# Two small pads that move the start addresses of an adaLN, convolution and bilinear-GLU kernel's tiles

## The chip, the cores and the metric

The kernel runs on one core of one Trainium2 chip. The metric is the device time of one execution in microseconds, the median of three runs. The core has five engines with queues of their own: TensorE (PE in the profile, and PEld for the loading of its stationary operand), VectorE (DVE), ScalarE (ACT), GpSimd (POOL) and SyncE (SP), which issues most of the transfers.

## The reference

The input `x` is `A_u`, 2048 tokens of 640 channels in float32. Six rows of 640 (`sa, ca, ga, sb, cb, gb`) come from a conditioning vector.

```python
mod = (_silu(c) @ w_mod).reshape(c.shape[0], 6, 1, -1)
h = _layernorm(x, axis=-1) * (1 + ca) + sa
x = x + ga * _A_ref(h, ...)      # a long convolution over the tokens, by FFT
h = _layernorm(x, axis=-1) * (1 + cb) + sb
x = x + gb * _B_ref(h, ...)      # ((h @ w_gate) * (h @ w_up)) @ w_down, 1536 wide
```

`_A_ref` builds, for each channel, a kernel of 2048 taps from 192 complex modes, and convolves the tokens with it (padded to 4096, by FFT), plus `u * Dskip`. `_B_ref` is the gated unit without a nonlinearity.

## The kernel before

The kernel has two stages on one program. The first, to about 433 us, builds the convolution's kernels (GpSimd, ScalarE and VectorE make sines, cosines and products, line 651 and line 733; TensorE sums over the modes, lines 747 and 762) and does the FFTs on TensorE (lines 784 to 939). The second, from about 507 us, is the gated unit. Between them lie the last channels and the first layer norms of the second stage.

The order of all instructions is written out by hand: `SCHED` holds the due time of each piece of the first stage, and the loops at the end of `tile_kernel` hold the order of the second. A tile of memory is taken from pools. Pools on the left side are stacked upwards, those opened with `side="right"` downwards from the top of the memory. `const` is the first pool on the left, so every later left tile begins above it: first `pk` and `pk1` (the kernel-generation tiles `EQ`, `LQ`, `RH`, `Pha`, `QtA` and others), and, when those are closed, `wp`, which `mk` takes from for the second stage (`xb`, `wga`, `wgb`, `wur`, `wsgh`, `wsgl`, `hh1`, `hl1`, `e` and some `a` tiles). On the right lie first the convolution's tiles (`t_tw`, `t_ti`, `shr`, `oneR`, `f16`, `gh`, `hf` and others), and, when these are closed, the pool `gp`, whose tiles are all taken at once in one loop (line 1336).

In the second stage the precision of float32 is made of pairs: `hilo` (line 994 and, on ScalarE, line 135) splits a value into a high part and a rest, each of type fp32r, whose names end in `h` and `l`. A product of two such pairs is three matmuls per block: high by high, rest by high, high by rest. There are two kinds of products, and each matmul loads its own 128 x 128 stationary operand (PEld) and then streams its moving operand:

- `prod` (line 1030): 512 tokens wide. Moving are the activations, stationary the weights. The gate and up projections share partial sums, so that each loop over one of 12 feature blocks has seven products: `y_1` (6 matmuls), `z_1` (9), `x_1` (6), `y_2` (6), `x_2` (9), `y_3` (9) and `z_2` (9), 54 in all, for 1024 tokens in two operands of 512. There are two halves with 12 such loops each. `x_1` and `x_2` read `hh1`, `hl1` (activations) and `wsgh`, `wsgl` (weights); the others read `sh`, `sl`, `hh2`, `hl2` and `wth`, `wtl`, `wsuh`, `wsul`. Two `x` products stand apart, in `u_gate` (line 1164), before the first loop. The trace leaves out buffer numbers, so `hh` in it is `hh1` or `hh2`.
- `down` (line 1457): the down projection, four blocks of 512 tokens with 12 steps each. A step has 24 matmuls, in turn 384 and 256 columns wide. Moving are the weights, in `wsgh` and `wsgl`; stationary are the activations, split into `e` for steps 0 and 1 of blocks 0 and 2, and else into parts of `sh`, `sl`, `hh2`, `hl2`, which are free again by then (`d_prep`, from line 1424 on).

```python
def prod(ps, ks):
    for n, (a, b) in enumerate(((0, 0), (1, 0), (0, 1))):
        for m, (w, k, x, l) in enumerate(ks):
            PE.matmul(ps, w[a][:, k], x[b][:, l], start=n == 0 and m == 0, stop=n == 2 and m == len(ks) - 1)
```

```python
if m < 2:
    AH[tb, f] = tuple(mk("e", [P, 512], F32, 4).bitcast(F32R) for _ in range(2))
```

While block 1 runs, transposes of the next tokens (line 1110) stand between its steps. Line 804 in the first stage is a matmul of fp32r tiles as well: `shr` and `oneR`.

Of the kernel before, what the change touches and what calls it, by code (L numbers as in the profile page):

```python
# [10 lines left out]
F32 = mybir.dt.float32  # L11
F32R = mybir.dt.float32r
# [7 lines left out]
P = 128  # L20
# [109 lines left out]
def tile_kernel(ctx: ExitStack, tc: tile.TileContext, I, out):  # L130
# [6 lines left out]
    const = ctx.enter_context(tc.tile_pool(name="const", bufs=1))  # L137
# [15 lines left out]
    for k in range(11):  # L153
        V.memset(shl[:, k : k + 1], k + 1)
    colT = const.tile([P, 10], F32, name="colT")
    ry = const.tile([P, 24], F32, name="ry")
    ry, rv = ry[:, 0:16], ry[:, 8:24]

    slot = {k: iter(v) for k, v in SLOT.items()}
# [1176 lines left out]
    for n, sh_, dt_, b_ in ([(f"a{j}", [P, 512], F32, 1) for j in range(10, 15)] + [(n, [P, 512], F32, 1) for n in TMP]  # L1336
                            + [(n, [P, 3, 512], F32R, 1) for n in H2] + [(n, [P, 9, 512], F32R, 1) for n in SX]
                            + [("tf", [P, 8, P], F32, 1), ("wth", [P, 8, P], F32R, 2), ("wtl", [P, 8, P], F32R, 2), ("wsuh", [P, 4, P], F32R, 2),
                               ("wsul", [P, 4, P], F32R, 2)] + [(f"a{j}", [P, 512], F32, 1) for j in (*range(5), *range(15, 24))]):
        FIRST[n] = gp.tile(sh_, dt_, name=n, bufs=b_)  # L1340
    ps_a = ctx.enter_context(tc.tile_pool(name="ps_a", bufs=1, space=PSUM))

# [284 lines left out]
```

## Time and profile before

| | us |
|---|---|
| median of three runs (lowest, highest) | 966.64 (965.85, 967.36) |
| the profiled execution | 967.17 |
| its span, first to last instruction | 965.3 |
| mean granted clock of TensorE | 0.976 |

Times in the views of the trace count from the span's start. In rows of the timeline, the first number is the start and the second the length of a run of like instructions; the lengths of matmuls overlap, since the next one starts while the last one drains, so that the pitch of matmuls is read from starts, not from lengths. In the chain in order of time the numbers are start and length of a piece of the chain that ended last.

### The profile page before, as it was taken

How to read it: one execution, taken by the hardware profiler on the slowest of the kernel's cores; microseconds unless marked ns; L12 is line 12 of the kernel's file. 1: busy time of each engine (PE TensorE's matmuls, PEld its weight loads, DVE VectorE, ACT ScalarE, POOL GpSimd, SP SyncE). 2: the span in 40 equal slices, each digit the busy share in tenths (PEclk: the TensorE clock that was granted, in tenths of full speed). 3: DMA queues.
4: the chain of work that ended last, by engine and by line, in shares of the span. 5: the costliest groups of instructions: out<-in, count | busy, mean ns of one | idle time of the engine just before them, and what ended most of it. 6: DMA issues, size and time to landing. Idle time of an engine off the chain costs nothing.

```text
span 965.3 us, 26463 instructions
## 1 busy us (share of the span) xinstructions
PE 867.6 (90%) x11070; PEld 719.7 (75%) x11070; DVE 746.2 (77%) x1301; ACT 575.9 (60%) x1088; POOL 568.1 (59%) x419
## 2 busy tenths in 40 slices
PE   3877887898798789889889999999999999999998
PEld 1665655676575467678567888899998888889998
DVE  7996687889789967887899777795677877677452
ACT  7899988887987979754773222235555222224330
POOL 5998999799799989940125766721021544451000
PEclk9978999999999889999999999999999999999999
DMA  8496575534465645468853355155536222213241
GB/s 302 153 305 220 163 235 187 135 122 126 122 189 166 178 118 156 137 206 265 226 162 110 108 191 171 48 197 158 192 137 218 83 82 82 82 55 90 74 165 55
DMA packets 141320, 148.94 MB, mean 154 GB/s; under 512 B 8208, under 2 KB 119568, under 8 KB 139792
## 3 DMA queue, kind: packets, MB, share of 16 engines
q1 hardware_dynamic: 139904, 145.80, 48.3%
q8 instruction: 87, 1.43, 0.6%
q10 hardware_dynamic: 1296, 1.44, 0.4%
q14 instruction: 33, 0.27, 0.1%
HBM read 108.36 MB, written 38.86 MB: 153 GB/s over the span
## 4 chain that ended last, share of the span: by engine, by line
PE 47%; DVE 5%; ACT 1%; issue 1%; DMA 1%; DVEq 0%; SPq 0%; ACTq 0%
PE pa L1030 28%; PE pa L1457 16%; PE psg L1030 1%; DMA wgb<-B_w_gate 1%; DVE st L1083 1%; DVE sl L994 1%; PE psg L1164 1%; PE psg L1110 0%; PE psg L1457 0%; DVE a L1149 0%; ACT wsgh L135 0%; ACT hh L135 0%; ACT xb L135 0%; DVE xb L1470 0%; DVE wsgl L994 0%
## 5 line engine op out<-in xcount | busy, mean ns | idle before, releaser
L651 POOL TENSOR_TENSOR EQ<-LQ,RH 128x1536 f32<-128x1536 f32 x40 | 124.3, 3108 | 0.2
L135 ACT ACTIVATE z<-pa 128x512 f32<-128x512 f32 x24 | 14.4, 599 | 169.2 <-PE pa L1030 121.9
L994 DVE TENSOR_TENSOR wsgl<-wga,wsgh 128x640 fp32r<-128x640 f32 x72 | 70.4, 981 | 47.9 <-ACT wsgh L135 47.9
L135 ACT ACTIVATE wsgh<-wga 128x640 fp32r<-128x640 f32 x72 | 52.3, 732 | 66.1 <-PE pa L1457 34.7
L1401 POOL TENSOR_TENSOR z<-z,s 128x512 f32<-128x512 f32 x24 | 34.2, 1426 | 89.7 <-DVE s L1400 89.7
L1006 POOL TENSOR_TENSOR tf<-wur,wgb 128x256 f32<-128x256 f32 x24 | 19.0, 790 | 97.7 <-DVE wtl L994 58.8
L651 POOL TENSOR_TENSOR EP<-LP,RH 128x768 f32<-128x768 f32 x40 | 65.8, 1655 | 10.2 <-DVE PtB L733 10.2
L1457 PE MATMUL pa<-wsgh,sh 128*128 128x384 f32 (+1 forms) x295 | 69.6, 314 | 0.0
L1457 PE MATMUL pa<-wsgl,sh 128*128 128x384 f32 (+1 forms) x295 | 69.2, 312 | 0.0
L1457 PE MATMUL pa<-wsgh,sl 128*128 128x384 f32 (+1 forms) x295 | 69.2, 312 | 0.0
L651 POOL TENSOR_TENSOR Pha<-LH,DH 128x1536 int32<-128x1536 int32 (+1 forms) x21 | 62.5, 2977 | 0.5 <-ACT tra L135 0.3
L651 POOL TENSOR_TENSOR Phb<-LH,DH 128x1536 int32<-128x1536 int32 x20 | 62.4, 3118 | 0.0
L733 DVE TENSOR_TENSOR QtA<-tra,EQ 128x1024 f32<-128x1024 f32 x44 | 51.9, 1215 | 9.8 <-ACT tra L135 6.8
L994 DVE TENSOR_TENSOR wtl<-tf,wth 128x256 fp32r<-128x256 f32 (+1 forms) x72 | 59.0, 845 | 0.0
L733 DVE TENSOR_TENSOR QtA<-trb,EQ 128x1024 f32<-128x1024 f32 x36 | 42.7, 1217 | 10.3 <-ACT trb L135 8.0
L1399 DVE TENSOR_TENSOR s<-pa,s 128x512 f32<-128x512 f32 x24 | 16.6, 690 | 43.9 <-PE pa L1030 38.9
L762 PE MATMUL kg<-QtB,PtB 64*32 64x64 f32 x2560 | 46.3, 222 | 4.5 <-issue 2.0
L762 PEld LDWEIGHTS kg<-QtB,PtB 64*32 64x32 f32 x2560 | 39.2, 110 | 12.4 <-issue 5.3
L1457 PEld LDWEIGHTS pa<-wsgh,sl 128*128 128x128 f32 x295 | 45.7, 188 | 0.0
L1457 PEld LDWEIGHTS pa<-wsgl,sh 128*128 128x128 f32 x295 | 45.7, 188 | 0.0
L1457 PEld LDWEIGHTS pa<-wsgh,sh 128*128 128x128 f32 x295 | 45.7, 188 | 0.0
L1030 PE MATMUL pa<-sh,wtl 128*128 128x512 f32 x144 | 44.9, 393 | 0.8 <-DVE wtl L994 0.8
(650 smaller groups left out, 2853.5 us busy)
## 6 DMA issues: line engine op xcount, KB each, us to landing
wga<-wdg SPq DMA_DIRECT2D x24, 640.0 KB, 4.3
wga<-B_w_gate SPq DMA_DIRECT2D x12, 640.0 KB, 5.9
wgb<-B_w_gate SPq DMA_DIRECT2D x24, 320.0 KB, 3.4
wur<-B_w_up SPq DMA_DIRECT2D x24, 320.0 KB, 4.0
xb<-x2d SPq DMA_DIRECT2D x6, 1280.0 KB, 8.5
t_ti<-w_mod SPq DMA_DIRECT2D x3, 1600.0 KB, 8.8
t_tw<-w_mod SPq DMA_DIRECT2D x3, 1600.0 KB, 10.4
WD<-Wa SPq DMA_DIRECT2D x8, 512.0 KB, 3.1
```

The costliest lines, as they stand in the source:

```text
L135: return S.activation(o, i, f, **kw)
L651: G.tensor_tensor(o.rearrange("p x (h l) -> p x h l", l=8), lo.unsqueeze(2).to_broadcast([P, rows, nh, 8]), hi.rearrange("p h x -> p x h") ...
L733: V.tensor_tensor(t, tr, e.unsqueeze(1).to_broadcast([P, 2, R, 32]), op=OP.mult)
L762: PE.matmul(kg[j * 32 : j * 32 + 32, dd, :], PtB[lo : lo + 64, c, r, :], QtB[lo : lo + 64, c, r, :], start=False, stop=dd == 7 and c == 1, ...
L994: V.tensor_tensor(lo, v, hi, op=OP.subtract)
L1006: G.tensor_tensor(t[:, 0:2], u[:, 0:2], g[:, 0:2], op=OP.subtract)
L1030: PE.matmul(ps, w[a][:, k], x[b][:, l], start=n == 0 and m == 0, stop=n == 2 and m == len(ks) - 1)
L1083: V.bn_stats(st[:, i, k, :], XB[tb][:, i, k * P : k * P + P])
L1164: PE.matmul(UX[i], WS[i][a][:, k], HX[0][b][:, k], start=k in (0, 2) and n == 0, stop=k in (1, 4) and n == 2)
L1399: V.tensor_tensor(S67[i], ps, S6[i], op=OP.add)
L1401: G.tensor_tensor(ZT[i], ZT[i], S67[i], op=OP.add)
L1457: PE.matmul(ACC[tb][t][c], x[:, ts], w[:, cs], start=st, stop=f == NF - 1 and n == 2 and (one or t % 2 == 1))
```

## The change

The tile `ry` in `const` grows from 24 to 48 float32 values per partition, 96 bytes more; its users read the same columns. A tile `gap` of 96 bytes is added at the end of the list of tiles of `gp`. Nothing reads or writes it.

```diff
@@ -153,7 +153,7 @@
     colT = const.tile([P, 10], F32, name="colT")
-    ry = const.tile([P, 24], F32, name="ry")
+    ry = const.tile([P, 48], F32, name="ry")
     ry, rv = ry[:, 0:16], ry[:, 8:24]
@@ -1336,7 +1336,7 @@
-                               ("wsul", [P, 4, P], F32R, 2)] + [(f"a{j}", [P, 512], F32, 1) for j in (*range(5), *range(15, 24))]):
+                               ("wsul", [P, 4, P], F32R, 2)] + [(f"a{j}", [P, 512], F32, 1) for j in (*range(5), *range(15, 24))] + [("gap", [P, 24], F32, 1)]):
         FIRST[n] = gp.tile(sh_, dt_, name=n, bufs=b_)
```

In the built programs the tiles begin, within a partition, at these bytes. The large tiles of a group agree modulo 128, those of the second stage modulo 256 too.

| tiles | before | after | modulo 128 (modulo 256) |
|---|---|---|---|
| left, first stage: `EQ`, first buffer | 38816 | 38912 | 32 (160) to 0 (0) |
| left, second stage: `wsgh`, first buffer | 45472 | 45568 | 32 (160) to 0 (0) |
| left, second stage: `hh1`; `e`, first buffer | 67232; 93856 | 67328; 93952 | 32 (160) to 0 (0) |
| `gp`: `sh` | 135136 | 135040 | 96 (224) to 0 (128) |
| `gp`: `wth`, first buffer | 176096 | 176000 | 96 (224) to 0 (128) |
| right, first stage: `shr` | 192576 | 192576 | 64 (64), unchanged |

## Prediction

> **What bounds the kernel now.** I read the page first, for its span and for the lines of the chain that ended last.
>
> ```profile
> span 965.3 us, 26463 instructions
> PE pa L1030 28%; PE pa L1457 16%; PE psg L1030 1%; DMA wgb<-B_w_gate 1%; DVE st L1083 1%; DVE sl L994 1%; PE psg L1164 1%; PE psg L1110 0%; PE psg L1457 0%; DVE a L1149 0%; ACT wsgh L135 0%; ACT hh L135 0%; ACT xb L135 0%; DVE xb L1470 0%; DVE wsgl L994 0%
> ```
>
> The chain lies on TensorE, in the products of the gate and up projections (line 1030, `prod`) and in the down projection (line 1457, `down`). Next I read the busy times by stage, cut where the chain changes line. The columns are PE, PEld, DVE, ACT, POOL, the granted clock, the DMA share and GB/s.
>
> ```profile
> 0.00:433.00 433.00, 348.11 (x7820) 265.78 (x7821) 360.16 (x625) 367.75 (x695) 387.09 (x247) 0.95 0.58 178
> 507.00:637.00 130.00, 129.51 (x567) 106.37 (x568) 103.49 (x148) 37.61 (x85) 85.25 (x76) 1.00 0.41 134
> 637.00:730.00 93.00, 92.71 (x631) 91.89 (x630) 67.70 (x143) 49.48 (x81) 18.16 (x15) 1.00 0.46 153
> 730.00:875.00 145.00, 145.00 (x636) 119.02 (x635) 111.20 (x164) 45.76 (x101) 64.74 (x63) 1.00 0.31 100
> 875.00:962.00 87.00, 86.33 (x577) 86.09 (x576) 40.69 (x64) 27.05 (x44) 1.31 (x2) 1.00 0.31 99
> ```
>
> The convolution stage (0 to 433 us) is shared: GpSimd is busiest (387 of 433 us), ScalarE and VectorE close behind. From 507 us to the end TensorE is busy without a pause, at the full granted clock, and DVE and GpSimd have room. TensorE's own waits from 507 to 960 us are these two in total:
>
> ```profile
> PE pa L1030 <- DVE s L1387: 0.8, 1, 0.8
> PE psg L1110 <- ACT xb L135: 0.3, 1, 0.3
> ```
>
> So in that half no transfer and no other engine decides the time, only how fast one matmul follows another. A faster VectorE, ScalarE or DMA there is worth nothing.
>
> **What the change moves.** No instruction, no wait and no shape changes; the order on each engine is the same, and only buffer numbers in names shift by one. What changes are start addresses, and the built program has them as the change says. Taken modulo 128, the tiles of the left stack (from the kernel-generation tiles to `xb`, `wga`, `wsgh`, `wsgl`, `hh1`, `hl1`, `e`) go from 32 to 0, and the tiles of the pool `gp` (`sh`, `sl`, `hh2`, `hl2`, `wth`, `wtl`, `wsuh`, `wsul`) from 96 to 0. The convolution's right-hand tiles stay at 64. Two things change for TensorE: the absolute start, and the offset between left and right tiles, which was 64 bytes and is now none (128 modulo 256).
>
> *Absolute start.* A start of 64 modulo 128 already occurs: `shr` and `oneR` in line 804 are fp32r tiles with 512 columns, as in line 1030. The first pair of matmuls after a pause shows the pitch of the first: here line 804 (start 64), then line 1164 (both operands at 32).
>
> ```profile
> 106.87 0.50 PE L804 MATMUL psfc<-shr,oneR 128*128 128x512 f32 x1 [1.08 <-ACT f16b L135]
> 107.20 0.40 PE L804 MATMUL psfb<-shr,oneR 128*128 128x512 f32 x1
> ```
> ```profile
> 488.49 0.50 PE L1164 MATMUL psg<-hl,wsgh 128*128 128x512 f32 x1 [1.33 <-DVE hl L1151]
> 488.82 0.39 PE L1164 MATMUL psg<-hh,wsgh 128*128 128x512 f32 x1
> ```
>
> Both are 0.33 us. A start at 64 instead of 32 buys a matmul nothing; I price the absolute start at 0. A start at 0 with such an operand is in no row, so this can fail (third rival).
>
> *Offset of the two tiles, in the down projection.* Each of its 48 steps (24 matmuls) reads the weights `wsgh`, `wsgl` (left) as the moving operand and the activations as the stationary one. In steps 0 and 1 of an even block the activations are in `e`, a left tile: offset none. In all others they are in `sh`, `sl`, `hh2`, `hl2`: offset 64. These rows are the starts of steps 0, 1, 2, 3 of the first block:
>
> ```profile
> 637.12 0.74 PE L1457 MATMUL pa<-wsgh,e 128*128 128x384 f32 x4
> 640.64 0.75 PE L1457 MATMUL pa<-wsgh,e 128*128 128x384 f32 x4
> 644.16 0.46 PE L1457 MATMUL pa<-wsgh,sh 128*128 128x384 f32 x2
> 647.76 0.47 PE L1457 MATMUL pa<-wsgh,sh 128*128 128x384 f32 x2
> ```
>
> A step takes 3.52 us with `e` and 3.60 us from the first one with `sh` on. The chain in order of time (start, length) shows how that goes on, and the timeline behind it the starts of steps 6 and 7 of the second block:
>
> ```profile
> 637.29 46.64 PE pa L1457 x312
> 684.36 3.46 PE pa L1457 x24
> 688.25 3.60 PE pa L1457 x24
> 723.73 3.45 PE pa L1457 x24
> 875.21 45.92 PE pa L1457 x307
> 957.85 1.42 PE pa L1457 x9
> ```
> ```profile
> 703.50 0.45 PE L1457 MATMUL pa<-wsgh,sh 128*128 128x384 f32 x2
> 706.94 0.45 PE L1457 MATMUL pa<-wsgh,sh 128*128 128x384 f32 x2
> ```
>
> 46.64 us is 2 x 3.52 + 11 x 3.60. From 875.21 to 957.85 is 82.64 us, or 2 x 3.52 + 21 x 3.60. In the second block, which transposes interrupt, three steps take 3.60 (the first at 688.25) and eight take 3.44 (the first at 684.36, the last at 723.73). So with offset 64 a step falls into one of two rhythms, 3.60 or 3.44 us, and keeps it; with offset none it ran at 3.52 all four times. If every step now runs at the offset-none rhythm: 35 x 0.08 us gained, 8 x 0.08 us lost, 2.80 - 0.64 = 2.16 us gained.
>
> *The offset in the gate and up products.* Here both operands of one matmul always come from the same side, but the products alternate sides: `x_1` and `x_2` read `hh`, `hl` with `wsgh`, `wsgl` (left), the others right tiles, so the weights that are loaded ahead change side at those seams. The rows are the starts of `x_1` one loop earlier, then `y_1`, `x_1`, `y_2`, `x_2`, `y_3`, `z_2`:
>
> ```profile
> 552.12 0.62 PE L1030 MATMUL pa<-hh,wsgh 128*128 128x512 f32 x2
> ...
> 561.07 0.62 PE L1030 MATMUL pa<-sh,wth 128*128 128x512 f32 x2
> ...
> 564.47 0.62 PE L1030 MATMUL pa<-hh,wsgh 128*128 128x512 f32 x2
> ...
> 565.84 0.62 PE L1030 MATMUL pa<-sh,wth 128*128 128x512 f32 x2
> ...
> 567.22 0.85 PE L1030 MATMUL pa<-hh,wsgh 128*128 128x512 f32 x3
> ...
> 569.28 0.62 PE L1030 MATMUL pa<-hh,wth 128*128 128x512 f32 x2
> ...
> 571.36 0.85 PE L1030 MATMUL pa<-sh,wsuh 128*128 128x512 f32 x3
> ```
>
> `y_1` and `z_1` (15 matmuls, right tiles after right tiles) take 3.40 us, 226.7 ns each. After each change of side the pitch is longer: `x_1` 1.37 / 6 = 228 ns, `y_2` 1.38 / 6 = 230, `x_2` 2.06 / 9 = 229, `y_3` 2.08 / 9 = 231. The even pitch starts after a change of side only gradually. Whole halves, from the chain:
>
> ```profile
> 507.49 125.72 PE pa L1030 x549
> 633.21 4.08 PE psg L1030 x18
> 730.62 140.51 PE pa L1030 x615
> 871.13 4.08 PE psg L1030 x18
> ```
>
> 129.80 us for 567 matmuls and 144.59 us for 633, 274.39 in all, 228.7 ns each. At 226.7 ns 1200 of them take 272.0 us. The excess is 2.4 us; a few tenths of it may be real waits (0.8 and 0.3 us above), so I take 2.0. Its bounds: 0 if the seams are not the cause, 2.4 if they are all of it.
>
> *Everything else, costed at nothing.* In the convolution stage the left tiles move from 32 to 0. The only shape that GpSimd runs on tiles of different starts is 128x512, at 64 (line 800) and at 96 (line 1363):
>
> ```profile
> L800 POOL TENSOR_TENSOR hfa<-hfa,f16a 128x512 f32<-128x512 f32 x2 | 2.6, 1303 | 0.0
> L1363 POOL TENSOR_TENSOR a<-a,a 128x512 f32<-128x512 f32 x2 | 2.6, 1291 | 14.5 <-ACT a L135 14.5
> ```
>
> 1303 against 1291 ns: the rounder start is not faster. Bounds from this one per cent of GpSimd's 387 us are 3.6 us either way; I take 0, since the sign is against a gain and both rows scatter. Stores and loads with rounder addresses lie under TensorE after 507 us, whose waits above name no transfer. The two new pieces hold no instruction.
>
> **The sum.** 2.16 + 2.0 = 4.2 us. The profiled execution took 967.17 us, 1.9 us of it outside its span of 965.3 us; it lies 0.5 us above the median of 966.64 us. From the median: 966.64 - 4.2 = 962.4 us. This stage's time passes straight to the end, since the chain is TensorE there. By its own bounds (2.16 alone, or 2.16 + 2.4, and three tenths of scatter) this case reaches from 961.8 to 964.8 us. A difference of 0.2%, 1.9 us, is about what a measurement can tell from none.
>
> **The rivals.** *Addresses don't matter to TensorE* (30%). The rhythms 3.60 and 3.44 occur with the same tiles and differ only in how the step began; then 3.52 too may be the rhythm left by the products before, and the slow seams may come from waits at a product's start. For it: lines 804 and 1164 pitch alike. Against it: all four `e` steps, in both halves, run at 3.52, and the change to 3.60 falls on the first step with `sh`. Time: 966.6 us, scattering as before (965.85 to 967.36). The Trainium skill speaks for this rival: SBUF — State Buffer, "Who interferes with whom", gives TensorE two independent read ports, one for the moving operand and one for weight loads, and has it wait for no one. By that rule no offset could matter; the trace's 3.52 against 3.60 us doesn't fit it well, but doesn't refute it.
>
> *The shorter rhythm everywhere* (11%). If aligned tiles always lead to the better rhythm, 35 steps gain 0.16 and four gain 0.08: 5.9 us. The same step per matmul (3.44 against 3.52 us is 3.3 ns for each of 24) on the 1266 matmuls of line 1030 (24 loops of 54, less 30 that stand in line 1164), beside the 2.0 us, gives 4.2 + 2.0. Total 12.1: 954.5 us.
>
> *The cost per matmul goes altogether* (4%). The steps at 3.44 us have 24 matmuls of 320 columns on average, 143.3 ns each; 512 columns take 226.7. A line through both has 0.434 ns a column and 4.3 ns per matmul besides. If a start at 0 removed those 4.3 ns everywhere, line 1030 would gain 1266 x (228.7 - 222.4) = 8.0 us and the down steps would take 3.33 us, 11.1 us less in all: 947.5 us. Against it: line 804 at start 64 shows none of it. The Trainium skill, TensorE: Matmul & The Clock Gate, "Wait — 56ns, not 53.3ns?", states about 215.7 ns back to back for 512 columns; an estimate by that page for line 1030 alone is 1266 x 13 ns, some 16 us. No run here shows such a pitch: the trace's best is 226.7.
>
> *Slower* (10%). After the change left tiles begin at 0 and right ones at 128 modulo 256. If TensorE's reads repeat over 256 bytes and not 128, the sides still differ, by another offset, and may settle worse: every down step at 3.60 (8 x 0.16 + 4 x 0.08 = 1.6 us more) and every product like `y_3`, 231.1 against 228.7 ns (1266 x 2.4 ns = 3.0 us). Time: 971.2 us. It decides against a gain when over half of the steps at 3.44 are lost and `y_1` and `z_1` no longer run at 226.7. Against it: same-side pairs, wherever they are, find 226.7.
>
> **How the numbers follow.** The forecast has 45%: 962.4 us. Of it some 4 in 100 end within 0.2% (above 964.7 us). Faster: 41 + 11 + 4 = 56%. Same: 30 + 4 = 34%. Slower: 10%. The range leaves out the slower case and the vanished cost per matmul (14% together), and reaches from the shorter rhythm, 954.5, to no change with its scatter, 967.6 us.
>
> **What would show it.** Right: steps of `down` all 3.52 us apart, no 3.60 and no 3.44; `x_1` to `x_1` of one loop 12.24 us instead of 12.35; the spans to 433 and to 507 us unchanged. Wrong: steps with `sh` still at 3.60 (addresses don't matter, or repeat over 256 bytes); a pitch below 226 ns in line 1030 (the absolute start counts after all); or a gain before 507 us, where I cost everything at nothing.

## The result and the profile after

The changed kernel took 962.04 us (median of 11 runs, 959.74 to 967.53); the kernel before, 966.72 us (11 runs, 964.17 to 969.59). The ratio is 0.994, its 95% interval 0.9918 to 0.9963: faster by 0.6%, that is by 3.6 to 7.9 us. The forecast was 962.4 us. The total is right; the way to it is partly another one, as the trace shows.

The page after has the span, and the chain that ended last, by line:

```profile
span 959.8 us, 26463 instructions
...
PE pa L1030 28%; PE pa L1457 15%; PE psg L1030 1%; DVE st L1083 1%; DVE sl L994 1%; PE psg L1164 1%; PE psg L1110 0%; PE psg L1457 0%; DMA TVb<-WD 0%; DVE a L1149 0%; ACT hh L135 0%; ACT xb L135 0%; DVE xb L1470 0%; SPq L919 0%; DVE wsgl L994 0%
```

The instructions are the same 26463, and the chain is still TensorE's. The profiled execution took 961.62 us at the same mean clock as before, 0.976. The chain in order of time (start, length), of after:

```profile
508.30 125.31 PE pa L1030 x549
637.69 44.89 PE pa L1457 x312
...
713.89 3.60 PE pa L1457 x24
...
729.18 140.06 PE pa L1030 x615
873.33 44.20 PE pa L1457 x307
...
952.61 1.42 PE pa L1457 x9
954.06 2.48 DVE xb L1470 x6
```

and the last line of the same view of before, for comparison:

```profile
959.30 2.48 DVE xb L1470 x6
```

I use one measure throughout: the *stretch* from the first product of the first loop (508.30) to the last additions on VectorE (954.06). It is 445.76 us after and 959.30 - 507.49 = 451.81 us before: 6.05 us less. The stretch is worth having because the part ahead of it scatters: the first loop's product begins between 504.84 and 514.45 us in the 14 profiled executions of this study, one for each kernel. Two of these kernels (before, and kick64 below) are alike up to there and still differ by 2.65 us. Layouts that should be alike agree in the stretch within 0.1 us (shown below).

Where the 6.05 us came from, piece by piece: the first run of down steps 46.64 to 44.89 us (1.75); the down steps of blocks 2 and 3, 82.64 us before and 952.61 - 873.33 = 79.28 after (3.36); the two halves of line 1030 with their tails, 129.80 to 637.69 - 508.30 = 129.39 (0.41) and 144.59 to 873.33 - 729.18 = 144.15 (0.44); the rest of block 1, 46.69 to 46.60 (0.09). The sum is 6.05.

The timeline of after has the starts of steps 0 to 3 of the first block:

```profile
637.53 0.75 PE L1457 MATMUL pa<-wsgh,e 128*128 128x384 f32 x4
...
641.05 0.75 PE L1457 MATMUL pa<-wsgh,e 128*128 128x384 f32 x4
...
644.57 0.46 PE L1457 MATMUL pa<-wsgh,sh 128*128 128x384 f32 x2
...
648.02 0.45 PE L1457 MATMUL pa<-wsgh,sh 128*128 128x384 f32 x2
```

The `e` steps are 3.52 us apart as before; the step with `sh` takes 3.45 where it took 3.60. The long runs agree: 44.89 us, 13 steps, is 2 x 3.52 + 11 x 3.44, and 79.28 us, 23 steps, is 2 x 3.52 + 21 x 3.44. One step in block 1 (713.89) is at 3.60. So of the steps with `sh` none settled at 3.52: they went to the shorter of the two rhythms that the kernel before had.

No other engine makes the difference in these steps. In the last steps of block 3, here of before and then of after, VectorE, ScalarE and GpSimd do nothing and the DMA engines almost nothing (the columns are those of the prediction's table):

```profile
951.00:958.00 7.00, 7.00 (x48) 7.00 (x47) 0.00 (x0) 0.00 (x0) 0.00 (x0) 1.00 0.01 2
```
```profile
945.00:952.00 7.00, 7.00 (x51) 7.00 (x50) 0.00 (x0) 0.00 (x0) 0.00 (x0) 1.00 0.01 2
```

TensorE alone is at work, at the full granted clock, and the step is still 3.60 us in the first window and 3.44 us in the second.

In line 1030 a part of the excess at the seams (the changes from a product with left tiles to one with right tiles, or back) stayed. Two starts of `x_1` one loop apart, and `y_2`, `x_2`, `y_3`, `z_2` of the second loop:

```profile
552.80 0.62 PE L1030 MATMUL pa<-hh,wsgh 128*128 128x512 f32 x2
...
565.08 0.62 PE L1030 MATMUL pa<-hh,wsgh 128*128 128x512 f32 x2
...
566.45 0.62 PE L1030 MATMUL pa<-sh,wth 128*128 128x512 f32 x2
...
567.82 0.85 PE L1030 MATMUL pa<-hh,wsgh 128*128 128x512 f32 x3
...
569.87 0.62 PE L1030 MATMUL pa<-hh,wth 128*128 128x512 f32 x2
...
571.91 0.84 PE L1030 MATMUL pa<-sh,wsuh 128*128 128x512 f32 x3
```

A loop takes 12.28 us: 12.35 before, 12.24 predicted. `x_1` and `y_2` still pitch at 1.37 / 6 = 228 ns; `y_3`, at 231 before, takes 571.91 - 569.87 = 2.04 us, 2.04 / 9 = 227 ns, the even pitch.

Ahead of the stretch nothing changed that can be told. The windows of after, to 433 us, in the same columns as before:

```profile
0.00:433.00 433.00, 346.92 (x7816) 264.18 (x7818) 359.83 (x625) 367.65 (x695) 386.80 (x247) 0.95 0.58 177
```

GpSimd is busy for 386.80 us against 387.09.

### The profile page after: what moved, and what is told of

It reads as the page before. It is cut to its first block, busy times and chain, and to the rows that moved or that the text cites. A ratio compares the mean times of both kernels' runs of the same rounds, so it can differ in the third digit from the quotient of the medians.

```text
span 959.8 us, 26463 instructions
## 1 busy us (share of the span) xinstructions
PE 860.5 (90%) x11070; PEld 713.3 (74%) x11070; DVE 746.7 (78%) x1301; ACT 575.6 (60%) x1088; POOL 567.5 (59%) x419
## 4 chain that ended last, share of the span: by engine, by line
PE 47%; DVE 5%; ACT 1%; issue 1%; DMA 0%; SPq 0%; DVEq 0%; ACTq 0%
PE pa L1030 28%; PE pa L1457 15%; PE psg L1030 1%; DVE st L1083 1%; DVE sl L994 1%; PE psg L1164 1%; PE psg L1110 0%; PE psg L1457 0%; DMA TVb<-WD 0%; DVE a L1149 0%; ACT hh L135 0%; ACT xb L135 0%; DVE xb L1470 0%; SPq L919 0%; DVE wsgl L994 0%
## 5 line engine op out<-in xcount | busy, mean ns | idle before, releaser
L1457 PE MATMUL pa<-wsgh,sh 128*128 128x384 f32 (+1 forms) x295 | 67.5, 308 | 0.0
L1457 PE MATMUL pa<-wsgh,sl 128*128 128x384 f32 (+1 forms) x295 | 67.0, 306 | 0.0
L1457 PE MATMUL pa<-wsgl,sh 128*128 128x384 f32 (+1 forms) x295 | 67.0, 306 | 0.0
```

The costliest lines, as they stand in the source:

```text
L1457: PE.matmul(ACC[tb][t][c], x[:, ts], w[:, cs], start=st, stop=f == NF - 1 and n == 2 and (one or t % 2 == 1))
```

## The experiments

All kernels but the last take the kernel before or after and change the pads (all128 and weights64 add one to another tile, `hr`), so that the groups of tiles begin elsewhere. "Distance" is the start of a matmul's stationary tile less that of its moving tile, modulo 256; in the down steps with `sh` that is right less left, 64 before and 128 after. The experiments ran on several chips, so a time is set beside that of the kernel before on the same chip. Three theories:

- *start*: tiles that begin at multiples of 128 bytes (or 64) are read better, as the change's words have it;
- *distance*: only the distance of the two tiles counts, and sets the rhythm of a step (the time from its start to the next one's, when steps follow each other without a break);
- *chance* or *entry*: 3.60 and 3.44 are two states of the same addresses, and how a step begins picks one.

First the two halves of the change, and two layouts that separate start from distance.

```diff
 gap_alone:      ry [P, 24] (as before), gap [P, 24]
 const_alone:    ry [P, 48], no gap
 apart128_at32:  ry [P, 24], gap [P, 48]
 apart0_at0:     ry [P, 48], gap [P, 56]
```

**gap_alone.** Left tiles at 160, right ones at 128, distance 224.

> The unused tile alone: left tiles keep their start at 32 modulo 128 (160 modulo 256), the tiles of gp start at 0 modulo 128 (128 modulo 256). Right minus left is 224 modulo 256, a distance in no run so far. Distance theory (what counts is the distance between the starts of the moving and the stationary tile, modulo 256, whatever the starts themselves): down steps with sh at one rhythm between 3.44 and 3.60 us, the same as in const_alone; steps with e stay at 3.52; the stretch from the first loop product to the last one's end between 445.8 us (after) and 451.8 us (before). Start theory (multiples of 128 count): only one of two operands starts evenly, half of the gain, some 449 us, and the even products (y, z) faster than the others. Chance theory (addresses don't count): no way to tell, any mixture of 3.44, 3.52 and 3.60.

**const_alone.** Left at 0, right at 224, distance 224 again.

> The wider constant tile alone: left tiles start at 0 modulo 256, the tiles of gp keep 96 modulo 128 (224 modulo 256). Right minus left is 224 modulo 256, as in gap_alone, with every start different. Distance theory: the same rhythms as gap_alone, step for step, within 0.02 us. Start theory: half of the gain again, but now x_1 and x_2 (left tiles) are the faster ones. Chance theory: a mixture that differs from gap_alone's.

Measured: 964.51 us, ratio 0.9966 (0.9942 to 0.9989), and 964.59 us, 0.9969 (0.9945 to 0.9992), both beside a before of 968.59. The chains, of gap_alone and of const_alone:

```profile
509.42 125.74 PE pa L1030 x549
639.25 45.53 PE pa L1457 x312
958.11 2.48 DVE xb L1470 x6
```
```profile
511.43 125.78 PE pa L1030 x549
641.29 45.53 PE pa L1457 x312
960.17 2.48 DVE xb L1470 x6
```

The two have no start in common and the same distance, and are alike to the hundredth: 45.53 us for the first steps (2 x 3.52 + 11 x 3.50), stretches of 448.69 and 448.74. Each half of the change alone gives half of the gain (3.1 of 6.05 us in the stretch). The start theory too expected half, so these two do not tell it from the distance theory; the next layout does.

**apart128_at32.** The distance of after, with no tile at a multiple of 64: left 160, right 32.

> No tile of the second stage starts at a multiple of 64: left tiles at 160 modulo 256 as before the change, the tiles of gp at 32 modulo 256 (the unused tile is 192 bytes). Right minus left is 128 modulo 256, as after the change. Distance theory: as after the change, down steps with sh at 3.44 us, with e at 3.52, stretch 445.8 us, time about 962 us. Start theory: as before the change, steps at 3.60 and 3.44, stretch 451.8 us, time about 966.7 us.

Measured: 962.61 us beside 968.59, ratio 0.9938 (0.9918 to 0.9958). The chain:

```profile
510.41 125.28 PE pa L1030 x549
639.78 44.89 PE pa L1457 x312
...
720.32 3.59 PE pa L1457 x24
724.35 3.60 PE pa L1457 x24
...
956.27 2.48 DVE xb L1470 x6
```

It repeats after: 44.89 us, line 1030 at 125.28 (125.31 after), a stretch of 445.86 (445.76). The start theory falls here: the gain needs no aligned tile.

**apart0_at0.** All tiles at 0, distance 0, the case that the prediction took the change for.

> All tiles of the second stage start at multiples of 256 (constant tile 96 bytes wider, unused tile 224 bytes). Right minus left is 0. Distance theory: every down step at the rhythm of the e steps, 3.52 us, and no change of distance at the seams of line 1030, so all its products at 226.7 ns a matmul (a loop of 54 in 12.24 us); stretch some 447.5 us. Start theory: at least as fast as after the change, steps at 3.44 us or less, stretch 445.8 us or less.

Measured: 963.63 us beside 968.59, ratio 0.9955 (0.9936 to 0.9975). The chain, and from the timeline two starts of `x_1`:

```profile
508.47 124.97 PE pa L1030 x549
637.52 45.76 PE pa L1457 x312
...
730.05 139.74 PE pa L1030 x615
...
956.29 2.48 DVE xb L1470 x6
```
```profile
552.80 0.62 PE L1030 MATMUL pa<-hh,wsgh 128*128 128x512 f32 x2
...
565.04 0.62 PE L1030 MATMUL pa<-hh,wsgh 128*128 128x512 f32 x2
```

Here the two marks that the prediction set for TensorE are met: 45.76 is 13 x 3.52, and a loop takes 12.24 us. The mean pitch in line 1030 is 226.9 ns (228.2 before). Mean pitch means, here and below, the mean of the intervals from one start to the next in that line, without those of 250 ns and more, which are pauses; the prediction's 228.7 has the pauses in it. The stretch is 447.82, a gain of 3.99 us where the sum said 4.2. The change that was made is better than that by 2.06 us, because of its down steps; in line 1030 it is worse.

**all128.** If 128 bytes apart is best in the down steps, it may be so in line 1030 too: weights at 224 and activations at 96, everywhere.

```diff
-    ry = const.tile([P, 24], F32, name="ry")
+    ry = const.tile([P, 40], F32, name="ry")
-            SMALL.append(wp.tile([P, 64], F32, name="hr"))
+            SMALL.append(wp.tile([P, 96], F32, name="hr"))
-                            + [("tf", [P, 8, P], F32, 1), ...
+                            + [("gap", [P, 32], F32, 1), ("tf", [P, 8, P], F32, 1), ...
```

> Every pair of a moving and a stationary tile in the second stage, at the seams too, lies 128 modulo 256 apart, and no start is a multiple of 64: wsgh, wsgl, wth, wtl, wsuh, wsul at 224, hh1, hl1, e, hh2, hl2, sh, sl at 96 modulo 256 (the constant tile 64 bytes wider, the tile hr 128 bytes wider, the unused tile of 128 bytes between sl and tf). Distance theory, as a law for both lines: the 3.3 ns a matmul that 128 gains over 0 in the down steps (3.44 against 3.52 us) come in line 1030 too, 226.7 to 223.3 ns, a loop of 54 in 12.06 us; e steps at 3.44; stretch 445.8 - 5.3 - 0.3 = 440.2 us, some 956.5 us. Narrower distance theory (226.7 ns is the floor for 512 columns, the distance only disturbs on top of it): line 1030 at 226.7 at best, stretch 444.5 us, some 961 us. Start theory: nothing is aligned, as before, 966.7 us.

Measured: 974.5 us beside 969.54, ratio 1.0056 (1.0035 to 1.0077), slower than before. The chain:

```profile
507.25 128.37 PE pa L1030 x549
639.81 46.79 PE pa L1457 x312
687.03 3.45 PE pa L1457 x24
...
927.01 2.88 PE pa L1457 x19
930.61 2.88 PE pa L1457 x19
...
964.45 2.48 DVE xb L1470 x6
```

The stretch is 457.20 us, 5.4 us longer than before's. Line 1030 has a mean pitch of 232.8 ns, and the down steps are at 46.79 / 13 = 3.60 us, `e` too, with the very distance that gave 3.44 in after; only in block 1, which transposes interrupt, they are at 3.44. So the distance theory is not enough either: at 128 there are two rhythms, as there are at 64.

**Other distances.** Five layouts, with one run each, fill the curve; the pads are `ry` / `gap` in float32 values per partition. Their stretches are compared, since one time tells little: apart192_at32 took 971.75 us, 4.6 us more than the profiled execution of before (967.17), with a stretch 2.4 us shorter, because its first loop began at 514.45 and not at 507.49. The expectations stand in the order apart64_at0, apart192_at32, apart96_at32, apart32_at0, apart160_at0.

> Left tiles at 0, tiles of gp at 64 modulo 256 (unused tile 160 bytes, constant tile 96 bytes wider): the distance 64 of before the change, with rounder starts. Distance theory: as before the change, steps with sh at 3.60 us in blocks 0, 2 and 3, and 3.60 or 3.44 in block 1; stretch 451.8 us. Start theory: the left half starts evenly, 449 us or less.

> Left tiles at 160, tiles of gp at 96 modulo 256 (unused tile 128 bytes, constant tile as before): distance 192, that is 64 the other way round. Distance theory with a sign (the stationary tile's place ahead of the moving one counts): a rhythm other than before's. Without a sign: 3.60 and 3.44 as before, stretch 451.8 us.

> Left tiles at 160, tiles of gp at 0 modulo 256 (unused tile 224 bytes, constant tile as before): distance 96. Known in down steps so far: 0 gives 3.52, 64 gives 3.60 or 3.44, 128 gives 3.44, 224 gives 3.50. Distance theory: one even rhythm, somewhere in 3.44 to 3.60 us, in steps with sh; e steps at 3.52. Start theory: half aligned as in gap_alone, 3.50.

> Left tiles begin at 0 and right ones at 32 modulo 256, 32 bytes apart. Distance theory (the distance of the moving from the stationary tile modulo 256 sets which rhythm a down step has): one rhythm for all steps with sh, between 3.44 and 3.60 us, 3.50 to 3.52 as at 96, 192 and 224; total 964 to 966 us. Start theory (the left start at 0 modulo 128 is what helps): 3.44 us and 962 us. If a distance that is no multiple of 64 bytes were bad in itself: 3.60 and 967 us or more.

> Left tiles begin at 0 and right ones at 160 modulo 256. Distance theory, with 96, 192 and 224 at 3.50 to 3.52 us and 128 at 3.44: one rhythm, 3.52 us, total 964 to 966 us. If the rhythm were a smooth curve around 128, 160 would lie at 3.46 to 3.48 us, total 963 us. Start theory (left start at 0): 3.44 us.

The column "us" mixes chips, on which the kernel before took 966.3 to 969.5 us, and medians with single runs; the last three columns are read from one trace each.

| kernel (`ry` / `gap`) | left, right, distance | us | step with `sh`, us | line 1030, mean ns | stretch, us |
|---|---|---|---|---|---|
| before (24 / none) | 160, 224, 64 | 966.72 | 3.60, some 3.44 | 228.2 | 451.81 |
| apart64_at0 (48 / 40) | 0, 64, 64 | 966.98 | 3.60, some 3.44 | 228.2 | 451.78 |
| after (48 / 24) | 0, 128, 128 | 962.04 | 3.44, one 3.60 | 227.5 | 445.76 |
| apart128_at32 (24 / 48) | 160, 32, 128 | 962.61 | 3.44, two 3.60 | 227.4 | 445.86 |
| apart0_at0 (48 / 56) | 0, 0, 0 | 963.63 | 3.52 | 226.9 | 447.82 |
| apart32_at0 (48 / 48) | 0, 32, 32 | 965.14 | 3.52 | 228.3 | 449.48 |
| apart96_at32 (24 / 56) | 160, 0, 96 | 965.38 | 3.52 | 228.7 | 449.89 |
| apart160_at0 (48 / 16) | 0, 160, 160 | 966.12 | 3.52 | 228.7 | 449.95 |
| apart192_at32 (24 / 32) | 160, 96, 192 | 971.75 | 3.52 | 228.2 | 449.42 |
| gap_alone (24 / 24) | 160, 128, 224 | 964.51 | 3.50 | 228.3 | 448.69 |
| const_alone (48 / none) | 0, 224, 224 | 964.59 | 3.50 | 228.4 | 448.74 |

A steady step in the chain of apart160_at0 (two pieces, whose starts are a step apart):

```profile
921.90 2.82 PE pa L1457 x19
925.42 2.82 PE pa L1457 x19
```

It takes 3.52 us. Two rhythms, 3.60 and 3.44, were seen only at 64 and 128; every other distance tried has one, 3.50 to 3.52. A smooth curve around 128 (3.46 to 3.48 at 160) is not there. Before and apart64_at0 lie 256 bytes apart in their whole distance (89664 and 89408 bytes between `wsgh` and `sh`) and agree within 0.03 us, so 256 is a period as far as this pair tells; 128 is not, since 0 differs from 128 and 64 from 192.

**weights64.** In line 1030 the layouts above have distance 0 inside a product and another one only at the seams. Here every pair is 64 apart, at the seams too, and the down steps are 192 apart, with `e` as well.

```diff
-    ry = const.tile([P, 24], F32, name="ry")
+    ry = const.tile([P, 40], F32, name="ry")
-            SMALL.append(wp.tile([P, 64], F32, name="hr"))
+            SMALL.append(wp.tile([P, 112], F32, name="hr"))
-                            + [("tf", [P, 8, P], F32, 1), ...
+                            + [("gap", [P, 16], F32, 1), ("tf", [P, 8, P], F32, 1), ...
```

> All six weight tiles of the loops begin at 224 and all activation tiles at 160 modulo 256: every pair of line 1030, seams too, is 64 bytes apart, and every pair of the down steps, with e too, 192 apart. Distance theory: down steps all 3.52 us; line 1030 has no seams of another distance, so its mean pitch is either at the floor of 226.7 ns (total 963 us) or, if 64 bytes apart within a product is bad as 128 was (232.8 ns), 229 to 233 ns (total 967 to 972 us). Side theory (seams alone cost): 226.7 ns. If addresses act only between tiles of one pool: as before, 228.2 ns and 966.7 us.

Measured: 971.48 us in one run (before beside it 966.33, one run too). Two starts of `x_1`, and the down steps in the chain:

```profile
553.90 0.63 PE L1030 MATMUL pa<-hh,wsgh 128*128 128x512 f32 x2
...
566.50 0.63 PE L1030 MATMUL pa<-hh,wsgh 128*128 128x512 f32 x2
```
```profile
508.30 128.36 PE pa L1030 x549
640.86 45.76 PE pa L1457 x312
...
963.60 2.48 DVE xb L1470 x6
```

A loop takes 12.60 us, 233.3 ns for each of 54 matmuls, though the distance is the same at the seams as inside a product; the stretch is 455.30 us, 3.5 us longer than before's. In apart0_at0 the side changes as often and costs nothing. So it is not the change of side that costs, but the distance of the two tiles; 0 is the best of the three tried inside a product of line 1030 (0, 64, 128). The down steps are at 3.52, as in apart192_at32.

**kick64.** Is the rhythm at one distance picked by how a step begins? The layout of before, with four transposes that nobody reads ahead of steps 2 and 7 of blocks 0 and 2.

```diff
         (ah, al), (dh, dl) = AH.pop((tb, f)), WD2.pop((tb, f))
+        if tb in (0, 2) and f in (2, 7):
+            kick = ps_g.tile([P, 512], F32, name="psg")
+            for t in range(4):
+                PE.transpose(kick[:, t * P : t * P + P], ident, ident)
```

> The layout of before (distance 64), and four 128-column transposes whose result nobody reads ahead of down steps 2 and 7 of blocks 0 and 2. Entry theory (at 64 and 128 bytes apart two rhythms exist, 3.60 and 3.44 us, and the state in which a step begins picks one): steps after a kick change, some of those in blocks 0 and 2 to 3.44 us, and keep it until the next kick; each that does gains 0.16 us against about 0.3 us for a kick. Pure distance theory: all steps with sh in blocks 0 and 2 stay at 3.60 us, with only the kicks added, total about 968 us.

Measured: 963.46 us in one run (before beside it 966.33, one run too). The chain; the lines shift by four, so that line 1461 is the old 1457:

```profile
504.84 125.69 PE pa L1030 x549
...
641.65 0.44 PE psg L1452 x4
642.09 17.21 PE pa L1461 x120
...
659.73 20.66 PE pa L1461 x144
...
878.98 17.21 PE pa L1461 x120
896.63 20.88 PE pa L1461 x139
...
955.68 2.48 DVE xb L1474 x6
```

With the addresses of before, five steps after the first kick take 17.21 / 5 = 3.44 us instead of 3.60, in both blocks, and so do six after the second kick of block 0 (20.66 / 6). The second kick of block 2 goes the other way: from 896.63 on the steps are at 3.60 to the end. So at distance 64 what goes ahead of a step can pick its rhythm, and the rhythm is then kept until something interrupts. The kernel before shows the same in its block 1: there four transposes stand ahead of each of the first steps, and steps of 3.46 and 3.60 us alternate (in the prediction's chain, those at 684.36 and 688.25 are two of them). 16 steps gained 0.16 us, 2.56, and four kicks cost 0.44 each, 1.76: 0.80 us net. The stretch is 450.84, 0.97 us shorter than before's. The total tells less: of the 3.71 us by which it lies under the profiled execution of before, 2.65 lie ahead of the first loop, which began at 504.84 and not at 507.49.

## Why the prediction was right, and where it was not

*What bounds the kernel: right.* The whole gain of the stretch lies in pitches on TensorE; its waits in the stretch are 0.8 and 0.4 us after and were 0.8 and 0.3 us before.

*Absolute start, priced at 0: right.* Before and apart64_at0 differ in every start of the second stage and by 0.03 us in the stretch; after and apart128_at32 by 0.10.

*Offset in the down projection: the mechanism was right in kind, its term mis-sized.* The step that failed is "If every step now runs at the offset-none rhythm". It held 128 modulo 256 for none. The runs tell these apart: at 0 a step takes 3.52 us, at 128 it takes 3.44 or 3.60. The term was 2.16 us and measured 1.75 + 3.36 + 0.09 = 5.20. That a step at 64 falls into one of two rhythms and keeps it was right, and kick64 shows it; that 128 has the same two, and that the steps would settle at the shorter, was not in the sum.

*Offset in the gate and up products: right for distance 0, not for this change.* The term was 2.0 us and measured 0.41 + 0.44 = 0.85. With distance 0 at the seams (apart0_at0) it is (125.72 + 140.51) - (124.97 + 139.74) = 1.52 us in the two long pieces of the chain alone, at 226.9 ns. The rest of the reasoning, that a change of side delays, was too narrow: apart0_at0 changes side as often without a delay, and weights64, with one distance at the seams and inside the products, is slow in all of them (233.3 ns).

*Everything else at 0: right as far as it shows.* GpSimd's busy time to 433 us is 0.3 us less of 387. A gain or loss smaller than the scatter of that half, some microseconds, can't be excluded.

*The sum.* 4.2 us forecast, 6.05 in the stretch; the two errors, 3.0 us too little and 1.2 too much, partly cancel, and the scatter ahead of the stretch (2.65 us between two kernels that are alike up to there) is of like size. That the median came within 0.4 us of the forecast is therefore partly luck. By its own marks (down steps all 3.52 us apart with no 3.44, a loop of 12.24 us) the account did not hold for this change: the steps are 3.44 us apart and the loop takes 12.28. Both 4.2 and 6.05 lie in the measured 3.6 to 7.9, so the total alone would have passed for a proof of the forecast's steps; only the starts in the trace tell the two apart.

*The rivals.* "Addresses don't matter" falls with gap_alone and const_alone, whose intervals lie below 1, and with the three pairs of layouts that share a distance and no start: their stretches agree within 0.1 us, while those of different pairs lie up to 6 us apart. The rule of the Trainium skill that spoke for it (SBUF — State Buffer, "Who interferes with whom"), two independent read ports for TensorE, leaves no room for such a difference. The runs show one, 3.44 to 3.60 us for a step and 226.7 to 233.3 ns for a matmul, with the same instructions; that the two reads themselves collide is not shown. "The shorter rhythm everywhere" came true in the down steps and not in line 1030. "The cost per matmul goes" falls: no run has a settled pitch below 226.7. "Slower" had the right premise, that 128 modulo 256 is not the same as none; a worse settled state exists (all128, weights64), but not in the layout of the change.

*What stays open.* Why a step that follows `e` at 3.52 takes up 3.60 at distance 64 and 3.44 at 128; why 224 gives 3.50 and not 3.52; why the steps of all128, all at distance 128, begin at 3.60; and what in TensorE or the memory depends on the distance, of which the trace has no record. That kick64 picks a rhythm was seen in one execution, and which kick leads to which is not explained.

## What to carry over

Where a matmul streams one tile while the next stationary tile is loaded from another, the distance of the two in memory is a free parameter, worth 0.6% here: try a few pads, and judge by the starts of a steady loop and not by the total, which here scattered by about as much as the effect. A round address is not the point, and the distance that gives the best rhythm for one shape of matmul (128 in the down steps) can be a bad one for another (0 was best for 512 columns). Like steps that run at two pitches are a sign of two stable states: before pricing a change by "the" pitch, count how many there are.

## What was not expected of the hardware

- TensorE with a weight load for each matmul has pitches that depend on the distance of the two tiles modulo 256 bytes. For 512 columns: 226.7 ns at 0 (apart0_at0), 232.8 at 128 (all128), 233.3 at 64 (weights64). For a step of 24: 3.52 us at 0, 32, 96, 160 and 192, 3.50 at 224, 3.44 or 3.60 at 64 and 128.
- The order of the distances differs with the shape: in line 1030, 64 and 128 are the two slow ones of the three tried inside a product, and in a down step they alone reach 3.44 us.
- Four transposes of 128 columns, 0.44 us, can switch the steps behind them from 3.60 to 3.44 us with the same addresses, or back to 3.60.
